# Sorting one batch's v in its natural layout and re-tiling it through DRAM

## The chip, the cores and the metric

The kernel runs on one core of a Trainium2 chip. The metric is the device time of one execution in microseconds. A core has five engines with instruction queues of their own: PE (matrix multiplication; PEld is its weight load), DVE (vector), ACT (scalar), POOL (which here builds a few masks and issues the loads) and SP (which here only issues DMAs). Sixteen DMA engines move the data. They serve two queues in this kernel: the one that POOL feeds (shown as q0, software_dynamic) and the one that SP feeds (q1, hardware_dynamic).

## The reference

Four batches of eight heads, 768 positions, head size 64. A small matrix per head is made doubly normalised (five rounds of exp, row sums, column sums) and mixes the eight 96-row blocks of k and of v; attention is then local to each block; the attended rows, all heads side by side (512 wide), go through a feed-forward layer with a squared ReLU.

```python
for _ in range(5):
    P = np.exp(P - P.max(-1, keepdims=True))
    P = P / (P.sum(-1, keepdims=True) + 1e-9)
    P = P / (P.sum(-2, keepdims=True) + 1e-9)
k_sorted = einsum('bhij,bhjcd->bhicd', P, k_b)     # k_b, v_b: 8 blocks of 96 rows
v_sorted = einsum('bhij,bhjcd->bhicd', P, v_b)
attn = softmax(q_b @ k_sorted^T / sqrt(64))        # within each block
x = (attn @ v_sorted), heads side by side          # 3072 x 512
out = relu(x @ w_in)**2 @ w_out                    # 512 -> 2048 -> 512
```

## The kernel before

**Work and batches.** The code counts batches from 0, so "the second batch" is `b == 1`. The attention of a batch runs in four units, one for each pair of heads (`hp` 0 to 3). The feed-forward layer (`ffn_unit`) runs in eight passes of 384 tokens, two for each batch: 64 "up" matmuls (L810, 128x384) in 16 chunks of four, each followed by a ReLU on ACT (L818) and a square on DVE (L821), and then 48 "down" matmuls (L838, 128x512) in 12 chunks of four, each third of them ending in a copy on ACT and a store.

**What a unit of batches 0 and 1 does.** `s_q` transposes q on PE (L461). `s_sort` sorts k and v by a matmul whose weights are the data (L510), which leaves both transposed. `s_sc` makes the scores (L550), ACT the exponentials. `s_vt` turns the sorted v back, so that positions lie on partitions, by eight 128x128 transposes on PE (L598) into `vs`, copied there by DVE. `s_av` multiplies by v (L731), and DVE divides by the sums (L741, L742) into `ao`. `s_xt` transposes the result into `xT`, for the first batch and the last unit of the second on PE (L779), otherwise by a transposing DMA from SP (L764).

**What batches 2 and 3 do.** `s_nat` sorts k and v by 32x32 tiles of PE: 16 matmuls (L632) for two pairs of heads, with weights `w_t` that `build_wt` makes (L406, L412, L419). The loads of k and v then have another layout (`kv_t`: 128 partitions with 1536 consecutive elements each, where the natural layout of `q_r`, `k_r`, `v_r` gives 384 elements in a run). The sorted v comes out with positions in the wrong place: it is copied to `vn`, written to DRAM (`v_way`, L656) and read back as `vblk` (L662), from where `s_av` takes it. The ring `rvb` has three such buffers, each for two units.

**The order.** `Plan` holds every operation with its engine, an assumed cost and its dependencies; `lay` and `lay_late` give the attention's PE operations due times in feed-forward chunks (`n_up` = 28 to a pass). `Plan.run` lists the operations, and each engine's queue is written in that order: PE, DVE, ACT and SP run theirs strictly in order. POOL's order is not written out by the plan; the tile framework sets it. Buffers of q, k and v (`ld` pool) are two of each, taken in turn: batch 2 gets those of batch 0, batch 3 those of batch 1, and a load waits until the last reader of its buffer is through. A load also waits for the eighth load before it.

```python
wr = plan.add("SP", 0.33, write, evs + [loaded(b)])
there = plan.add("WAY", 2.0, lambda e: None, [wr])
rd = plan.add("SP", 0.33, read, [there] + oldw)
back = plan.add("WAY", 2.0, lambda e: None, [rd])
```

Of the kernel before, what the change touches and what calls it, by code (L numbers as in the profile page):

```python
# [11 lines left out]
ALU = mybir.AluOpType  # L12
# [116 lines left out]
def kernel(  # L129
# [103 lines left out]
    for n in range(3):  # L233
        vb_r.append(const.tile([96, NB, HP, 66], BF16, name=f"vblk{n}"))
    v_way = nc.dram_tensor("v_way", (B, 2, NA, 128, HP * 66), BF16, kind="Internal").ap()

    kn_r = [const.tile([128, NA, 2, D], BF16, name=f"kn{n}") for n in range(3)]
    qi_r = [const.tile([128, NA, 2, D], BF16, name=f"qi{n}") for n in range(2)]
# [13 lines left out]
    xT = const.tile([128, KC, n_tok], BF16)  # L252
    w_all = const.tile([128, NH // 2, NB, C0], BF16)
    w_t = const.tile([128, NH // 4, 4, NB], BF16)
    qkv = {}
    landed = {}

# [9 lines left out]

    def alloc_qkv(b):
        if b not in qkv:
            qkv[b] = [ld.tile([128, H, NA * D], BF16, tag=t, name=t) for t in ("qb", "kb", "vb")]  # L270

    def load(b, t, h0, n, p=slice(0, 128)):
        def dst_src():
            alloc_qkv(b)
            if b > 1 and t:
                return (qkv[b][t].rearrange("p (g h) x -> p g (h x)", h=HP)[:, h0 // HP, :],
                        kv_t[t][b, :, h0 // HP, :])
            return qkv[b][t][p, h0:h0 + n, :], (q_r, k_r, v_r)[t][b, p, h0:h0 + n, :]
        dma((b, t, h0, p.start), 1.57 * n / H * (p.stop - p.start) / 128, dst_src,
            readers[b - 2] + [x_done[b - 1, x, 0] for x in range(HP)] if b > 1 else [])  # L280

    def load_w_in(g):
        f = slice(d_ff // 4 * g, d_ff // 4 * (g + 1))
# [23 lines left out]
    load_w_in(0)  # L307
    for g in range(1, 4):
        load_w_in(g)
    for g in range(4):  # L310
        t = slice(NT // 4 * g, NT // 4 * (g + 1))
        dma(("w_out", g), 1.05, lambda t=t: (w_out_bf[:, t, :], w_out_r[:, t, :]))
    for g in range(2):
        for t in (2, 1, 0):
            load(1, t, HP * g, HP)


    rs = const.tile([NH, NB], FP32)
# [83 lines left out]
    def build_wt(due):  # L402

        st = {}
        pick = const.tile([128, NB, 4], BF16, name="pick")
        picked = plan.add("DVE", 0.2, lambda e: nc.vector.tensor_copy(  # L406
            out=pick, in_=ident.rearrange("p (j c) -> p j c", c=C0)[:, :, 0:4]), [x_done[0, HP - 1, 0]])

        def mm(e):
            st["p"] = ps1.tile([128, NB, NH // 4], FP32, tag="p1", name="wtp")  # L410
            for h in range(4):
                nc.tensor.matmul(  # L412
                    out=st["p"][32 * h:32 * (h + 1), :, :].rearrange("p i g -> p (i g)"),
                    lhsT=pick.rearrange("p j c -> p (j c)"),
                    rhs=pt.rearrange("p i (g h) -> p h i g", h=4)[:, h, :, :],
                    start=True, stop=True)

        def fn(e):
            nc.vector.tensor_tensor(  # L419
                out=w_t,  # L420
                in0=mask_t[:, None, :, None].to_broadcast([128, NH // 4, 4, NB]),
                in1=st["p"].rearrange("p i g -> p g i")[:, :, None, :]
                .to_broadcast([128, NH // 4, 4, NB]),
                op=ALU.mult)

        s1, old = r1.take()
        pe = plan.add("PE", 0.15, mm, [cp, picked] + old, due, mode="col32")
        built["t"] = plan.add("DVE", 0.45, fn, [pe])
        r1.use(s1, pe, built["t"])


    class Unit:
# [184 lines left out]
    def s_nat(b, g, t, due):  # L617

        if t == 2:
            m, oldm = rvn.take()  # L620
        evs = []
        for hp in (2 * g, 2 * g + 1):
            slot, old = r2.take()
            if t == 1:
                m, oldm = rkn.take()

            def mm(e, hp=hp, slot=slot):
                src = qkv[b][t].rearrange("p (g h) x -> p g (h x)", h=HP)
                for h in range(2):
                    r = slice(32 * (2 * (hp % 2) + h), 32 * (2 * (hp % 2) + h + 1))  # L630
                    for c in range(4):
                        nc.tensor.matmul(  # L632
                            out=p2[slot][32 * c:32 * (c + 1), h, 0:NA * D],
                            lhsT=w_t[r, HP // 2 * b + g, :, :].rearrange("p c i -> p (c i)"),
                            rhs=src[r, g, NA * D * c:NA * D * (c + 1)],
                            start=True, stop=True, tile_position=(r.start, 32 * c))

            def ev(e, hp=hp, slot=slot, m=m):
                dst = (vn_r[m][:, :, 2 * (hp % 2):2 * (hp % 2) + 2, 0:D] if t == 2
                       else kn_r[m])  # L640
                copy(e, dst, p2[slot][:, :, 0:NA * D].rearrange("p e (a d) -> p a e d", d=D))

            pe = plan.add("PE", 0.15, mm, [landed[b, t, HP * g, 0], built["t"]] + old, due,
                          mode="tile")
            readers[b].append(pe)
            op = plan.add(AD, cost_f(2 * NA * D), ev, [pe] + oldm)
            r2.use(slot, pe, op)
            evs.append(op)
            if t == 1:
                rkn.use(m, op)  # L650
                k_nat[b, hp] = m, op
        if t == 1:
            return

        def write(e):
            nc.sync.dma_start(out=v_way[b, g].rearrange("a p x -> p a x"),  # L656
                              in_=vn_r[m].rearrange("p a h x -> p a (h x)"))

        w, oldw = rvb.take()

        def read(e):
            nc.sync.dma_start(  # L662
                out=vb_r[w].rearrange("p i h x -> p (i h x)"),
                in_=v_way[b, g].rearrange("a (c i) x -> (a c) (i x)", i=NB))

        wr = plan.add("SP", 0.33, write, evs + [loaded(b)])
        there = plan.add("WAY", 2.0, lambda e: None, [wr])
        rd = plan.add("SP", 0.33, read, [there] + oldw)
        back = plan.add("WAY", 2.0, lambda e: None, [rd])
        rvn.use(m, *evs, there)  # L670
        rvb.use(w, back)
        v_blk[b, g] = w, back
# [41 lines left out]

    def s_av(u, due=0):
        nao, olda = rao.take()
        if u.b > 1:
            w, u.vs_op = v_blk[u.b, u.hp // 2]
        u.norms = []
        for hf in u.halves:  # L720
# [4 lines left out]
            def mm(e, hf=hf, st=st, slot=slot):  # L725
                if hf == u.halves[0]:
                    u.ao = att.tile([96, u.ni, 2, D], BF16, tag="ao", name="ao", bufs=3)
                st["p"] = oup = p2[slot]
                for n in range(NQ):
                    for h in range(2):  # L730
                        nc.tensor.matmul(  # L731
                            out=oup[:, h, 66 * n:66 * n + D + 1],
                            lhsT=et_r[u.et[hf]][:, h, BLK * n:BLK * n + 128],
                            rhs=(u.vs[:, NQ * hf + n, h, 0:D + 1] if u.b < 2 else
                                 vb_r[w][:, NQ * hf + n, 2 * (u.hp % 2) + h, 0:D + 1]),
                            start=True, stop=True)

# [13 lines left out]
            op = plan.add("DVE", 0.9, norm, [pe])  # L751
            r2.use(s2, pe, op)
            ret.use(u.et[hf], pe)
            if u.b < 2:
                rks.use(u.n, pe)
            else:
                rvb.use(w, pe)
# [179 lines left out]
    def lay(b, halves, c0, c1):  # L937
        step, gap = (c1 - c0) / (HP + 0.9), (c1 - c0 - 13) / (HP - 1)
        for hp in range(HP):
            c = c0 + step * hp  # L940
            box = {}

            def open_(due, b=b, hp=hp, box=box):
                u = box["u"] = Unit(b, hp, halves)
                u.q_op = q2ops[hp] if b == 0 else s_q(b, hp, 0, 128, due)
                if b == 1:
                    build_w(H * b + 2 * hp, 2, pt, kops[b - 1, hp])
                u.k_op = kops[b, hp] = s_sort(u, 1, due)
                u.v_op = s_sort(u, 2, due)

            for f, s in ((0.0, open_),
                         (0.35, lambda due, box=box: s_sc(box["u"], due)),
                         (0.5, lambda due, box=box: s_vt(box["u"], due)),
                         (0.75, lambda due, box=box: s_av(box["u"], due)),
                         (1.2, lambda due, box=box: s_xt(box["u"], due))):
                todo.append((c + step * f, len(todo), s, b))

    def lay_late(b, c0):

        todo.append((c0, len(todo), lambda due: load_late(b), 0))  # L960
        if b == 2:
            todo.append((c0, len(todo), build_wt, 0))
        for g in range(2):
            for t in (1, 2):
                todo.append((c0 + 9 + 9 * g, len(todo),
# [17 lines left out]
                load(b, t, HP * g, HP)  # L983

    lay(0, (1,), 0, n_up)
    lay(1, (0, 1), n_up, 2 * n_up)
    lay_late(2, 2 * n_up)
    lay_late(3, 4 * n_up)
# [45 lines left out]
```

The softmax here doesn't subtract the row's maximum and nothing guards it: scores larger than these inputs give would overflow.

## Time and profile before

| what | value |
|---|---|
| median of 3 runs | 226.49 us (226.41 to 226.63) |
| the profiled execution's own time | 226.45 us |
| its span, first to last instruction | 224.3 us (2.15 us lie around it) |
| PE busy in the span | 216.6 us (97%) |
| PEld, ACT, DVE busy | 122.9, 122.1, 105.7 us |
| POOL busy | 26.4 us |
| granted PE clock | 1.00 throughout |
| DMA, mean over the span | 129 GB/s, 28.83 MB |

PE is busy in nearly all of the span; the other engines are busy for about half of it. The page cuts the span into 40 slices of 5.6 us; in its DMA row a 9 stands where the sixteen DMA engines are busy all the time. The first feed-forward pass begins at 22.3 us, the third (the first of the second batch) at 82.6 us. Between 49.4 and 82.5 us PE interleaves the second batch's attention with the second feed-forward pass.

### The profile page before, as it was taken

The numbers are of one execution on the slowest core, as the hardware profiler recorded it, in microseconds if no ns is written. First come the engines' busy times: TensorE is split into PE (matmuls) and PEld (weight loads), VectorE is DVE, ScalarE is ACT, GpSimd is POOL, SyncE is SP. The second block draws the span as 40 slices with busy tenths as digits, with TensorE's granted clock in tenths as the row PEclk, the third lists the DMA queues.
The fourth block names the chain that finished last, engine by engine and source line by source line (L and its number), as shares of the span: only waits on it lengthen the run. The fifth ranks groups of instructions, "written<-read, shape, count | busy, mean of one in ns | idle before, by whom it ended". The sixth has DMA issues, their size and how long they took to land.

```text
span 224.3 us, 5245 instructions
## 1 busy us (share of the span) xinstructions
PE 216.6 (97%) x2130; PEld 122.9 (55%) x2145; DVE 105.7 (47%) x297; ACT 122.1 (54%) x253; POOL 26.4 (12%) x46
## 2 busy tenths in 40 slices
PE   7898999999999999999999999999999999999994
PEld 2476665556665645545665455445665465446553
DVE  6777777317666416640666127523664045005400
ACT  4665776228885328734775248535774177137521
POOL 7962332200004200000000000000000000000000
PEclk9999999999999999999999999999999999999999
DMA  5999999999953996499941320899522410110012
GB/s 66 201 202 208 207 206 205 203 227 245 210 65 27 191 239 145 115 216 201 220 38 35 85 94 0 164 225 254 110 37 43 122 47 1 50 57 37 0 50 94
DMA packets 42744, 28.83 MB, mean 129 GB/s; under 512 B 22752, under 2 KB 38368, under 8 KB 42720
## 3 DMA queue, kind: packets, MB, share of 16 engines
q0 software_dynamic: 13888, 13.63, 37.1%
q1 hardware_dynamic: 28832, 14.86, 29.7%
q8 instruction: 17, 0.28, 0.5%
q14 instruction: 7, 0.06, 0.1%
HBM read 28.89 MB, written 7.91 MB: 164 GB/s over the span
## 4 chain that ended last, share of the span: by engine, by line
PE 92%; DMA 2%; DVE 2%; ACT 1%; issue 1%; ACTq 0%; POOLq 0%
PE hp L810 37%; PE op L838 35%; PE p L550 4%; PE p L731 3%; DMA qb<-in_q_dram 2%; PE p L510 2%; PE qtp L461 2%; PE vbp L598 2%; PE op L872 2%; PE p L350 1%; PE p L632 1%; PE xtp L779 1%; PE tp L510 1%; DVE ao L742 1%; ACT h L818 0%
## 5 line engine op out<-in xcount | busy, mean ns | idle before, releaser
L810 PE MATMUL hp<-xT,w_in_bf 128*128 128x384 bf16 x512 | 91.0, 326 | 0.0
L838 PE MATMUL op<-w_out_bf,h 128*128 128x512 bf16 x353 | 82.6, 379 | 0.8
L818 ACT ACTIVATE h<-hp 128x384 bf16<-128x384 f32 x128 | 62.0, 495 | 23.5 <-PE hp L810 20.0
L821 DVE TENSOR_TENSOR h<-h 128x384 bf16<-128x384 bf16 x128 | 44.5, 355 | 56.3 <-ACT h L818 55.5
L810 PEld LDWEIGHTS <-w_in_bf 128*128 128x128 bf16 x512 | 47.0, 98 | 30.0 <-issue 0.7
L838 PEld LDWEIGHTS <-h 128*128 128x128 bf16 x368 | 34.7, 98 | 39.4 <-issue 0.7
L192 ACT COPY ob<-op 128x512 f32<-128x512 f32 (+1 forms) x25 | 14.2, 569 | 56.0 <-PE op L838 50.6
L742 DVE TENSOR_TENSOR ao<-p,rec 96x512 bf16<-96x512 f32 x32 | 22.0, 687 | 1.4 <-DVE rec L741 0.3
L582 ACT ACTIVATE et<-p 96x384 bf16<-96x384 f32 x48 | 19.4, 491 | 2.4 <-PE p L550 2.4
L741 DVE RECIPROCAL rec<-p 96x8 f32<-96x8 f32 x32 | 6.4, 199 | 13.6 <-PE p L731 13.3
L731 PEld LDWEIGHTS <-et 96*128 96x128 bf16 x256 | 10.6, 97 | 2.9
L261 POOL DMA_DIRECT2D qb<-in_q_dram x8 | 6.0, 754 | 32.5 <-PE qtp L461 24.4
L350 PE MATMUL p<-ones 128*128 128x512 bf16 (+1 forms) x36 | 8.8, 360 | 1.1 <-DVE ones L213 1.1
L194 DVE COPY vs<-vbp 96x512 bf16<-96x512 bf16 (+1 forms) x12 | 6.1, 508 | 7.1 <-PE vbp L598 6.9
L573 ACT ACTIVATE et<-p 96x768 bf16<-96x768 f32 x8 | 6.3, 802 | 2.1 <-PE p L550 2.0
L261 POOL DMA_DIRECT2D kb<-in_k_dram x10 | 6.6, 659 | 6.6 <-DMA w_in_bf<-in_moe_w_in_dram 2.2
L261 POOL DMA_DIRECT2D vb<-in_v_dram x10 | 6.6, 660 | 6.4 <-DMA w_in_bf<-in_moe_w_in_dram 3.6
L192 ACT CAST ksT<-p 128x768 bf16<-128x768 f32 (+1 forms) x7 | 4.6, 662 | 3.3 <-PE p L510 3.3
L550 PEld LDWEIGHTS <-kx 64*128 64x128 bf16 x128 | 4.6, 155 | 2.8 <-issue 2.8
L731 PE MATMUL p<-vs,et 96*128 96x65 bf16 x128 | 6.0, 193 | 0.0
L461 PE MATMUL qtp<-ident,qb 64*64 64x64 bf16 (+1 forms) x144 | 4.7, 204 | 1.3 <-DMA qb<-in_q_dram 1.3
L461 PEld LDWEIGHTS <-qb 64*64 64x64 bf16 (+1 forms) x144 | 3.5, 109 | 4.5 <-DMA qb<-in_q_dram 2.3
(78 smaller groups left out, 129.3 us busy)
## 6 DMA issues: line engine op xcount, KB each, us to landing
out_dram<-ob SPq DMA_DIRECT2D x23, 256.0 KB, 2.8
qb<-in_q_dram POOLq DMA_DIRECT2D x8, 384.0 KB, 15.7
vb<-in_v_dram POOLq DMA_DIRECT2D x6, 384.0 KB, 17.1
kb<-in_k_dram POOLq DMA_DIRECT2D x6, 384.0 KB, 17.1
w_in_bf<-in_moe_w_in_dram POOLq DMA_DIRECT2D x4, 512.0 KB, 12.5
w_out_bf<-in_moe_w_out_dram POOLq DMA_DIRECT2D x4, 512.0 KB, 18.0
v_way<-vn SPq DMA_DIRECT2D x4, 396.0 KB, 4.1
vblk<-v_way SPq DMA_DIRECT2D x4, 396.0 KB, 3.9
```

Of the source, the lines that this page charges most:

```text
L192: nc.scalar.copy(out=out, in_=in_)
L261: nc.gpsimd.dma_start(out=dst, in_=src)
L350: nc.tensor.matmul(out=out, lhsT=ones, rhs=rhs, start=True, stop=True)
L461: nc.tensor.transpose(out=t["p"][64 * h:64 * (h + 1), a, :], in_=qb[p0:p1, 2 * hp + h, D * a:D * (a + 1)], identity=ident[p0:p1, p0:p1])
L550: nc.tensor.matmul(out=scp[:, h, BLK * n:BLK * (n + 1)], lhsT=(u.ksT[64 * h:64 * (h + 1), hf, BLK * n:BLK * n + 128] if u.b < 2 else kx_r[ ...
L582: nc.scalar.activation(out=et[:, h, 0:HS].rearrange("p (n c a) -> p n c a", c=C0, a=NA), in_=st["p"][0:96, h, 0:HS].rearrange("p (n a c) - ...
L731: nc.tensor.matmul(out=oup[:, h, 66 * n:66 * n + D + 1], lhsT=et_r[u.et[hf]][:, h, BLK * n:BLK * n + 128], rhs=(u.vs[:, NQ * hf + n, h, 0: ...
L742: nc.vector.tensor_tensor(out=u.ao[:, n0:n0 + NQ, :, :].rearrange("p n e d -> p e n d"), in0=ov[:, :, :, 0:D], in1=rec[:, :, :, None].to_b ...
L810: nc.tensor.matmul(out=t["hp", nt][:, 0:HS], lhsT=w_in_bf[:, kc, 128 * nt:128 * (nt + 1)], rhs=xT[:, kc, t0:t0 + HS], start=(kc == 0), sto ...
L818: nc.scalar.activation(out=t["h1", nt], in_=t["hp", nt][:, 0:HS], func=AF.Relu)
L821: nc.vector.tensor_tensor(out=t["h2"][:, nt, :], in0=t["h1", nt], in1=t["h1", nt], op=ALU.mult)
L838: nc.tensor.matmul(out=t["op", mt], lhsT=t["h2"][:, nt, 128 * mt:128 * (mt + 1)], rhs=w_out_bf[:, nt, :], start=(nt == 0), stop=(nt == NT ...
```

## The change

The second batch's v (its k stays as it was) goes the way of batches 2 and 3:

- `load`: v of batch 1 comes in the `kv_t` layout. Its first half is loaded between `w_in` and `w_out`, the rest of batch 1 in the order v, k, q, k, q after `w_out`.
- `build_wt` runs in the first feed-forward pass (it ran just before the third) and makes a second, small set of weights `w_v` for it (one more DVE instruction).
- `s_nat(1, g, 2)` runs for g = 0 and 1 in the first feed-forward pass, due in chunks 14 and 24. It replaces, in the four units of batch 1, the sort of v (`s_sort(u, 2)`) and `s_vt`.
- The sorted v is written to `v_nat` in DRAM by four DMAs for each g (32 partitions with 3168 bytes in one piece each) and read back to `vblk` by one DMA for each g (96 partitions x 8 pieces of 528 bytes). The plan assumes 6 us for each way, 2 us for the later batches' `v_way`.
- `s_av` of batch 1 takes v from `vblk`. The ring `rvb` now serves batches 1, 2 and 3.
- Buffers of q, k, v: batch 2 now takes those of batch 1 and batch 3 those of batch 0. In the built program POOL's queue has, after batch 1's loads, first the six loads of batch 3 (q, q, k, v, k, v), then batch 2's (v, v, q, q, k, k). Before, batch 2's six loads (q, q, k, v, k, v) stood ahead of batch 3's.

```diff
+    v_nat = nc.dram_tensor("v_nat", (B, 2, NB, BLK, HP * 66), BF16, kind="Internal").ap()
...
+    w_v = const.tile([128, 2, NB, 4], BF16)
...
     def alloc_qkv(b):
         if b not in qkv:
-            qkv[b] = [ld.tile([128, H, NA * D], BF16, tag=t, name=t) for t in ("qb", "kb", "vb")]
+            m = (b + 1) // 2 % 2
+            qkv[b] = [ld.tile([128, H, NA * D], BF16, tag=f"{t}{m}", name=t, bufs=1)
+                      for t in ("qb", "kb", "vb")]
...
-            if b > 1 and t:
+            if b > 1 and t or b == 1 and t == 2:
...
-            readers[b - 2] + [x_done[b - 1, x, 0] for x in range(HP)] if b > 1 else [])
+            readers[(0, 0, 1, 0)[b]] + [x_done[b - 1, x, 0] for x in range(HP)] if b > 1 else [])
...
+    load(1, 2, 0, HP)
     for g in range(4):
         t = slice(NT // 4 * g, NT // 4 * (g + 1))
         dma(("w_out", g), 1.05, lambda t=t: (w_out_bf[:, t, :], w_out_r[:, t, :]))
-    for g in range(2):
-        for t in (2, 1, 0):
-            load(1, t, HP * g, HP)
+    for t, g in ((2, 1), (1, 0), (0, 0), (1, 1), (0, 1)):
+        load(1, t, HP * g, HP)
...
+        built["v"] = plan.add("DVE", 0.25, fn1, [pe])
...
+                w = (w_v[:, g, :, :].rearrange("p i c -> p (i c)") if b == 1 else
+                     w_t[:, HP // 2 * b + g, :, :].rearrange("p c i -> p (c i)"))
...
+                            lhsT=w[r, :],
...
+            for c in range(4):
+                nc.sync.dma_start(
+                    out=v_nat[b, g].rearrange("i (y z a) x -> z (i y) (a x)", z=4, a=NA)[c],
+                    in_=vn_r[m][32 * c:32 * (c + 1)].rearrange("p a h x -> p (a h x)"))
...
+            if b == 1:
+                nc.sync.dma_start(
+                    out=vb_r[w].rearrange("p i h x -> p i (h x)"),
+                    in_=v_nat[b, g].rearrange("i p x -> p i x"))
+                return
...
-        wr = plan.add("SP", 0.33, write, evs + [loaded(b)])
-        there = plan.add("WAY", 2.0, lambda e: None, [wr])
+        wr = plan.add("SP", 0.33, write, evs + ([loaded(b)] if b > 1 else []))
+        slow = 6.0 if b == 1 else 2.0
+        there = plan.add("WAY", slow, lambda e: None, [wr])
...
-        if u.b > 1:
+        if u.b > 0:
             w, u.vs_op = v_blk[u.b, u.hp // 2]
...
-                u.v_op = s_sort(u, 2, due)
-
+                if b == 0:
+                    u.v_op = s_sort(u, 2, due)
+
+            if b == 1 and hp % 2 == 0:
+                todo.append((14 + 5 * hp, len(todo),
+                             lambda due, g=hp // 2: s_nat(1, g, 2, due), b))
...
-                         (0.5, lambda due, box=box: s_vt(box["u"], due)),
+                         (0.5, lambda due, box=box: b == 0 and s_vt(box["u"], due)),
...
-        if b == 2:
-            todo.append((c0, len(todo), build_wt, 0))
...
+    todo.append((8, len(todo), build_wt, 0))
```

More of the change, by code (lines that the diff above doesn't have):

```diff
@@ L424, in fn, with fn1 @@
                 op=ALU.mult)
+        def fn1(e):
+            nc.vector.tensor_tensor(
+                out=w_v,
+                in0=mask_t[:, None, None, :].to_broadcast([128, 2, NB, 4]),
+                in1=st["p"][:, :, 2:4].rearrange("p i g -> p g i")[:, :, :, None]
+                .to_broadcast([128, 2, NB, 4]),
+                op=ALU.mult)
         s1, old = r1.take()
         pe = plan.add("PE", 0.15, mm, [cp, picked] + old, due, mode="col32")
+        built["v"] = plan.add("DVE", 0.25, fn1, [pe])
         built["t"] = plan.add("DVE", 0.45, fn, [pe])
-        r1.use(s1, pe, built["t"])
+        r1.use(s1, pe, built["v"], built["t"])
     class Unit:
@@ L633, in mm @@
                             out=p2[slot][32 * c:32 * (c + 1), h, 0:NA * D],
-                            lhsT=w_t[r, HP // 2 * b + g, :, :].rearrange("p c i -> p (c i)"),
+                            lhsT=w[r, :],
                             rhs=src[r, g, NA * D * c:NA * D * (c + 1)],
@@ L655, in write @@
         def write(e):
-            nc.sync.dma_start(out=v_way[b, g].rearrange("a p x -> p a x"),
-                              in_=vn_r[m].rearrange("p a h x -> p a (h x)"))
+            if b > 1:
+                nc.sync.dma_start(out=v_way[b, g].rearrange("a p x -> p a x"),
+                                  in_=vn_r[m].rearrange("p a h x -> p a (h x)"))
+                return
[3 more added lines that the diff above has]
+                    in_=vn_r[m][32 * c:32 * (c + 1)].rearrange("p a h x -> p (a h x)"))
         w, oldw = rvb.take()
         def read(e):
+            if b == 1:
+                nc.sync.dma_start(
+                    out=vb_r[w].rearrange("p i h x -> p i (h x)"),
+                    in_=v_nat[b, g].rearrange("i p x -> p i x"))
+                return
             nc.sync.dma_start(
@@ L664, in read @@
                 in_=v_way[b, g].rearrange("a (c i) x -> (a c) (i x)", i=NB))
-        wr = plan.add("SP", 0.33, write, evs + [loaded(b)])
-        there = plan.add("WAY", 2.0, lambda e: None, [wr])
+        wr = plan.add("SP", 0.33, write, evs + ([loaded(b)] if b > 1 else []))
+        slow = 6.0 if b == 1 else 2.0
+        there = plan.add("WAY", slow, lambda e: None, [wr])
         rd = plan.add("SP", 0.33, read, [there] + oldw)
-        back = plan.add("WAY", 2.0, lambda e: None, [rd])
+        back = plan.add("WAY", slow, lambda e: None, [rd])
         rvn.use(m, *evs, there)
@@ L733, in mm @@
                             lhsT=et_r[u.et[hf]][:, h, BLK * n:BLK * n + 128],
-                            rhs=(u.vs[:, NQ * hf + n, h, 0:D + 1] if u.b < 2 else
+                            rhs=(u.vs[:, NQ * hf + n, h, 0:D + 1] if u.b < 1 else
                                  vb_r[w][:, NQ * hf + n, 2 * (u.hp % 2) + h, 0:D + 1]),
@@ L753, in s_av @@
             ret.use(u.et[hf], pe)
-            if u.b < 2:
+            if u.b < 1:
                 rks.use(u.n, pe)
```

## The prediction

> **What bounds the kernel now.** I read the busy row first, then the slices, then the chain of work that ended last.
>
> ```profile
> PE 216.6 (97%) x2130; PEld 122.9 (55%) x2145; DVE 105.7 (47%) x297; ACT 122.1 (54%) x253; POOL 26.4 (12%) x46
> PE   7898999999999999999999999999999999999994
> DMA  5999999999953996499941320899522410110012
> PE 92%; DMA 2%; DVE 2%; ACT 1%; issue 1%; ACTq 0%; POOLq 0%
> ```
>
> PE is the bound: from 22 us on it hardly idles, so PE time removed there comes off the end, and any wait of PE adds to it. But the DMA row is full of 9s for the first 11 slices, up to 62 us: this is where the change puts its way through DRAM. Next, PE in order of time over one unit of the second batch:
>
> ```profile
> 49.75 0.50 PE L510 MATMUL p<-w_all,kb 128*64 128x128 bf16 x12
> 50.08 0.50 PE L510 MATMUL p<-w_all,vb 128*64 128x128 bf16 x12
> 50.52 1.47 PE L810 MATMUL hp<-xT,w_in_bf 128*128 128x384 bf16 x8
> 51.92 0.51 PE L550 MATMUL p<-qT,ksT 64*128 64x96 bf16 x16
> 52.37 0.62 PE L598 MATMUL vbp<-ident,vsT 128*128 128x128 bf16 x8
> 52.83 1.46 PE L810 MATMUL hp<-xT,w_in_bf 128*128 128x384 bf16 x8
> ```
>
> The first column is the start; a step's cost is the distance to the next start (ends overlap). Last, the packets of the two queues in two short windows (queue: packets, MB, share of 16 engines), 46.5 to 47 us and 60.5 to 60.75 us:
>
> ```profile
> q1 hardware_dynamic: 51, 0.10, 61.0%
> q0 software_dynamic: 54, 0.04, 51.1%
> ...
> q0 software_dynamic: 18, 0.05, 93.7%
> q1 hardware_dynamic: 19, 0.00, 12.4%
> ```
>
> With both queues filled the packets alternate one to one, whatever their size: 2 KB stores (q1) with 768-byte loads, then 256-byte transposes (q1) with 3 KB loads.
>
> **PE time removed.** Sort of v: 50.08 to 50.52, 56.93 to 57.39, 64.00 to 64.46, 70.54 to 71.00. The first counts 0.33 only (k followed by v takes 0.33, k followed by feed-forward 0.44), so 0.33+3x0.46 = 1.71 us. Turning v back: 0.46, 0.45, 0.45, 0.67 (73.28 to 73.95); where the scores were followed by it directly (first and last unit) they took 0.45, followed by feed-forward 0.64, so 2.03-2x0.19 = 1.65 us. Together 3.36.
>
> **PE time added.** Two sorts by tiles: 16 such matmuls of batch 2 stood for 0.31 us (88.57 to 88.88) to 0.53, and the eight up matmuls ahead of them took 1.40 instead of 1.30; 0.42 each, 0.84 (up to 1.26). The weights' four matmuls (82.45 to 82.61) only move. By the built order the last unit's q and k no longer stand together: 0.1. Net 2.4; I take 2.3 (1.7 to 2.5), as the weights' PSUM buffer is now the one that the next `vbp` needs, behind two DVE steps (`w_t` 0.42, `w_v` less): up to 0.3 wait.
>
> **What is costed at nothing.** DVE and ACT lose four casts of `vsT` and four copies of `vs` (0.69 each) and get four casts of `vn` (0.96 on DVE, 0.80 on ACT); the first pass gets some 2.5 us more of both together, where each is busy for 11 of 15 us (22 to 37 us) and three PSUM buffers lie between them and PE; without that cover 0.3. `w_out` lands one load later, its last quarter at 39.5 instead of 37.6 us; the fourth chunk of down matmuls reads it at 41. Batch 2's loads now come last on POOL, q and k only after the second batch's q transposes and k sorts (70.0 and 70.3 before, some 72 to 75 in my case): keys land by 83, and the tile sort needs them 6 us into the third pass, at 90. SP's queue gets ten DMAs ahead of the second batch's transposes into `xT`; the third pass needs these at 82.6 before, 85 in my case.
>
> **The way through DRAM, the term that decides.** Per DMA engine, a 768-byte packet takes 0.059 us (1064 in 37.6 to 41.5 us over 16 engines), a 3 KB packet 0.24 (77 in 57 to 58 us, ten of them tiny), a small packet alone 0.029 (552 of 256 bytes in 65 to 66 us). A load is 32 packets per engine in natural layout (1.9 us) or 8 of 3 KB (1.9 us). A read of `v_nat` is 96x8/16 = 48 per engine: 1.4 us alone, 48x(0.059+0.029) = 4.2 beside natural loads, 48x(0.24+0.029) = 12.9 beside 3 KB loads. A DMA of SP issued into a full q0 also starts late: the store issued at 42.77 has its first packets after 46.0, and the three stores of that stretch take 5.3 to 6.5 us to land, where one at 128 us takes 2.8. I take 3.0 us to the first packet (rows 2.4 to 3.4).
>
> First half: `vn` is ready near 37, written by 44, the read is issued at 44, starts at 47 behind a store, lands at 52.5. Its `s_av` stood at 54.13; +1.0 (weights and two tile sorts), -0.33 and -0.27 removed ahead: 54.5. It fits by 2 us.
>
> Second half: `vn` is ready at 48; the write stands in SP's queue behind that read and a store, ends at 55, lands at 55.5; the read is issued at 56, first packets at 59. POOL's queue then: batch 1's last load lands near 52.5 (49.99 before, plus what SP's packets take), batch 3's two q by 59. Behind them stand six 3 KB loads without a break (batch 3's k, v, k, v, batch 2's v, v): 6x8 = 48 packets per engine, as many as the read has. Turn by turn both end together: 59 + 48x0.27 = 71.5 us. It cannot be much later, because q0's next loads wait for PE. The third unit's `s_av` needs it: 68.27 before, +1.0, -1.25 and -1.17 for three units' steps, -0.65 because one chunk less stands ahead of it: 66.2. PE, which runs in order, waits 5.3 us. With the 2.4 us start the read lands at 69.7 and the wait is 3.5. I take 4.6 (3.5 to 6), near the 3.0 row, three stores against one transpose. Behind the waiting matmul stand all feed-forward chunks.
>
> **A cold PE.** After such a wait PE may run slowly for a while. The trace has this only at its start: 512-column matmuls of 634 ns at first and 379 later, the first six or seven 0.43 us apart instead of 0.22, which loses 1.4 us. Later idle times are at most 1.34 us and cost nothing of the kind. So 0 to 1.4; I take 1.0, nearer to the row with a long idle time ahead. [...]
>
> [...] The two windows above show one to one in the trace's own packets, so my sum goes by the rows.
>
> **Sum.** Against the profiled execution's 226.45 us (its own span 224.3 and 2.15 around it; the median 226.49 is the same within 0.02%): -2.3 +4.6 +1.0 = 229.75; I say 229.7. A measurement of this kernel can tell about 0.2%, 0.45 us, from no change.
>
> **Rivals.**
> 1. The second read is in time (528-byte pieces take several to a turn, or q0 is a load further on). PE's saving stays: 226.45-2.3 = 224.1 (223.9 to 224.8). For it: the first read has this outcome by my own sum, and each us by which the read starts earlier, still beside natural loads, lets it land 3 us earlier (11 packets more, 0.27 each later). Against it: the alternation above and 48 packets each. It decides from a first packet before 57.5. Chance 0.23.
> 2. The read is nearly in time, but the transposes into `xT` (3x48 packets per engine, issued at 57 to 68, beside the same 3 KB loads) are the late ones: the first began 3.7 us after its issue and took 7.1 to land even with q0 about to run dry. Not stopped by an earlier wait, the third pass would need them at 80 while q0 stays full to 83: a wait of 1 to 3.5 us. 225.2 to 227.7, about no change. Chance 0.12, half of it within 0.2%.
> 3. My case with a bigger loss: batch 2's keys late as well, from the point where they land after 90 us instead of 83, or both reads late: 231 to 233. Chance 0.05.
>
> **How the numbers follow.** My case, 0.60: saving 1.7 to 2.5, wait 3.5 to 6, cold 0 to 1.4: its own range 227.5 to 231.6. With rival 1's 224.1 the range has to reach to 224.0, since leaving that case out loses 0.23; it leaves out most of rival 3 and the edges. Faster: rival 1 and a part of rival 2, 0.25. Same: 0.07. Slower: 0.60+0.05 and the rest of rival 2, 0.68.
>
> **What would show it.** Right: in the waits, PE at `s_av` of the second batch waits once for the DMA `vblk<-v_nat`, 3.5 to 6 us, near 66 us; that read takes 13 to 16 us to land, the other 8 to 9; the first 512-column matmuls after it are slower; the slices near 66 us show PE at 1 to 4. Then from the third pass on the timeline is that of before, shifted by 2 to 4 us. Wrong: both reads land in under 10 us and PE has no wait over 1 us (rival 1), or PE's wait stands at the first L839 up matmuls of the third pass (rival 2), or at the tile sort of k (rival 3).

## The result, and the profile after

The changed kernel takes **232.12 us** (median of four runs, 231.59 to 232.76); the kernel before takes 226.56 us beside it (226.41 to 226.92). The ratio is 1.0244, with a 95% interval of 1.0212 to 1.0276: slower by 5.6 us. The forecast was 229.7 us with a range from 224.0 to 231.6: the direction and the place of the wait are right, and the time lies 2.4 us above the forecast and 0.5 us above its range.

The profiled execution took 232.76 us; its span is 230.6 us. From the page: the busy row, the slices (5.77 us each), and the chain that ended last.

```profile
PE 219.4 (95%) x2097; PEld 121.5 (53%) x2097; DVE 103.7 (45%) x294; ACT 121.6 (53%) x253; POOL 26.0 (11%) x46
PE   8998999999955999999999999999999999999994
PEclk9999999999996799999999999999999999999999
DMA  5999999999997992079963221499921410011012
PE 79%; DMA 14%; DVE 3%; ACT 1%; issue 1%; SPq 1%; POOL 0%; ACTq 0%; DVEq 0%; POOLq 0%
```

PE has fewer instructions (2097 for 2130; the trace of before lacks 15 of its 368 down matmuls) but more busy time. Its row now has two 5s (63 to 75 us); the second of these slices and the one behind it have a lower granted clock. The DMA row is full up to 69 us, where it was full up to 62 before. The chain, almost all PE before, now goes through DMAs for 14%. PE's waits (total us, times, longest us):

```profile
PE p L760 <- DMA vblk<-v_nat: 5.2, 1, 5.2
PE p L355 <- DVE ones L213: 1.1, 1, 1.1
```

The second wait stands at the kernel's start, as before. The first is the new one. The timeline of PE (start, us): one unit of the second batch, the place of the wait, and the start of the third pass:

```profile
51.59 0.50 PE L524 MATMUL p<-w_all,kb 128*64 128x128 bf16 x12
52.03 1.48 PE L839 MATMUL hp<-xT,w_in_bf 128*128 128x384 bf16 x8
53.43 0.51 PE L564 MATMUL p<-qT,ksT 64*128 64x96 bf16 x16
53.88 1.47 PE L839 MATMUL hp<-xT,w_in_bf 128*128 128x384 bf16 x8
...
65.14 1.47 PE L839 MATMUL hp<-xT,w_in_bf 128*128 128x384 bf16 x8
71.85 1.04 PE L760 MATMUL p<-vblk,et 96*128 96x65 bf16 x16 [5.23 <-DMA vblk<-v_nat]
72.82 0.85 PE L475 MATMUL qtp<-ident,qb 128*64 128x128 bf16 x12
73.60 1.46 PE L839 MATMUL hp<-xT,w_in_bf 128*128 128x384 bf16 x4
74.85 1.91 PE L867 MATMUL op<-w_out_bf,h 128*128 128x512 bf16 x4
...
88.72 6.01 PE L839 MATMUL hp<-xT,w_in_bf 128*128 128x384 bf16 x36
```

In the unit the sort of v behind that of k and the eight transposes behind the scores are gone. `s_av` of the third unit (L760) begins at 71.85 us, after the second read of `v_nat`. The four up matmuls behind it take 1.46 us, where eight took 1.47 before the wait. The third pass begins at 88.72 us (82.61 before). From there to the end it is 141.9 us, and 141.7 before: all that changed lies ahead of it.

Packets of the two queues while the read waits, from 63 to 64 us (queue: packets, MB, share of 16 engines):

```profile
q0 software_dynamic: 59, 0.18, 88.1%
q1 hardware_dynamic: 58, 0.03, 14.6%
```

And from 71 to 72 us, when q0 has run dry (only q1 is listed, and what it moves by then are mostly the 256-byte packets of the transposes into `xT`):

```profile
q1 hardware_dynamic: 747, 0.19, 89.8%
```

58 of the read's 528-byte packets in a microsecond beside 59 of POOL's loads, 747 small ones alone: one to one, as in the windows of before (51 to 54, 19 to 18). Equal numbers alone would also come of longer turns of equal length; the start times of the packets decide it. From 63 to 68.5 us the commonest distance between the starts of two 3 KB packets is 0.266 us. From 60.9 to 62.3 us, when SP's queue moves nothing, it is 0.229 us. So between two 3 KB packets there are 0.037 us more: room for one small packet (58 of them in 14.6% of 16 us are 0.040 us each), and no more.

### The profile page after: what moved, and what is told of

It is laid out like the page before. It is cut to its first block, busy times and chain, and to the rows that moved or that the text cites. A ratio compares the mean times of both kernels' runs of the same rounds, so it can differ in the third digit from the quotient of the medians.

```text
span 230.6 us, 5180 instructions
## 1 busy us (share of the span) xinstructions
PE 219.4 (95%) x2097; PEld 121.5 (53%) x2097; DVE 103.7 (45%) x294; ACT 121.6 (53%) x253; POOL 26.0 (11%) x46
## 4 chain that ended last, share of the span: by engine, by line
PE 79%; DMA 14%; DVE 3%; ACT 1%; issue 1%; SPq 1%; POOL 0%; ACTq 0%; DVEq 0%; POOLq 0%
PE op L867 33%; PE hp L839 31%; DMA vblk<-v_nat 5%; DMA v_nat<-vn 4%; PE p L564 3%; PE p L760 3%; DMA qb<-in_q_dram 3%; DMA kx<-kn 2%; PE p L649 2%; PE op L901 2%; DVE ao L771 1%; PE p L524 1%; PE vbp L612 1%; PE qtp L475 1%; PE xtp L808 1%
## 5 line engine op out<-in xcount | busy, mean ns | idle before, releaser
L867 PE MATMUL op<-w_out_bf,h 128*128 128x512 bf16 x368 | 85.0, 383 | 0.0
L847 ACT ACTIVATE h<-hp 128x384 bf16<-128x384 f32 x128 | 61.3, 497 | 23.1 <-PE hp L839 18.8
L850 DVE TENSOR_TENSOR h<-h 128x384 bf16<-128x384 bf16 x128 | 44.2, 355 | 62.3 <-ACT h L847 61.2
L192 ACT COPY ob<-op 128x512 f32<-128x512 f32 (+1 forms) x24 | 13.6, 567 | 56.3 <-PE op L867 53.7
L760 PEld LDWEIGHTS <-et 96*128 96x128 bf16 x256 | 10.9, 99 | 8.5 <-issue 5.6
L760 PE MATMUL p<-vblk,et 96*128 96x65 bf16 x192 | 8.5, 197 | 5.3 <-DMA vblk<-v_nat 5.2
L355 PE MATMUL p<-ones 128*128 128x512 bf16 (+1 forms) x36 | 10.0, 399 | 1.1 <-DVE ones L213 1.1
L192 ACT COPY qT<-qtp 128x384 bf16<-128x384 bf16 (+1 forms) x11 | 5.7, 555 | 6.5 <-PE qtp L475 6.5
L263 POOL DMA_DIRECT2D vb<-in_v_dram x10 | 6.1, 613 | 10.3 <-DMA qb<-in_q_dram 4.1
L194 DVE CAST vn<-p 128x768 bf16<-128x768 f32 x6 | 5.7, 958 | 2.1 <-PE p L649 1.9
L564 PE MATMUL p<-qT,kx 64*128 64x96 bf16 x128 | 5.6, 226 | 0.0
L724 DVE COPY qi<-qb 128x768 bf16<-128x768 bf16 x8 | 2.7, 356 | 6.4 <-DMA qT<-qi 6.4
```

Of the source, the lines that this page charges most:

```text
L192: nc.scalar.copy(out=out, in_=in_)
L263: nc.gpsimd.dma_start(out=dst, in_=src)
L355: nc.tensor.matmul(out=out, lhsT=ones, rhs=rhs, start=True, stop=True)
L564: nc.tensor.matmul(out=scp[:, h, BLK * n:BLK * (n + 1)], lhsT=(u.ksT[64 * h:64 * (h + 1), hf, BLK * n:BLK * n + 128] if u.b < 2 else kx_r[ ...
L760: nc.tensor.matmul(out=oup[:, h, 66 * n:66 * n + D + 1], lhsT=et_r[u.et[hf]][:, h, BLK * n:BLK * n + 128], rhs=(u.vs[:, NQ * hf + n, h, 0: ...
L847: nc.scalar.activation(out=t["h1", nt], in_=t["hp", nt][:, 0:HS], func=AF.Relu)
```

## The experiments

The theory: two losses. PE waits 5.4 us for the second read, because six 3 KB loads stand in q0 beside it; and the clock that falls during this wait (0.50 for 6.83 us) costs more after it. The rivals: the clock costs nothing beyond the wait (the rest is another wait or the buffers' exchange); and the read is slow by itself.

**e2: keep PE busy in the wait.** 24 matmuls of 512 columns, whose result nobody reads, ahead of the waiting `s_av`.

```diff
+                if u.b == 1 and u.hp == 2 and hf == 0:
+                    fill(8.0, slot)
```

> Changed kernel with 24 dummy 512-column matmuls on PE (5.2 us, on data that nobody reads) ahead of the third unit's s_av, where PE waited 5.2 us for the read of v_nat. My theory (PE's wait costs 5.4 us, and the 6.83 us at half clock behind it another 3.4): the read lands when it did, near 71.7 us, PE's granted clock stays 1.00, time 232.1-3.4 = 228.7 us (228.2 to 229.2). Rival, the clock after the wait costs little and the rest of the loss lies elsewhere (the third pass's transposes, the loads of batch 2): 231 to 232.

Measured: 229.69 us (229.53 to 230.03), ratio 1.0143 (1.0128 to 1.0159). PE's timeline:

```profile
66.42 5.34 PE L355 MATMUL p<-ones 128*128 128x512 bf16 x24
71.60 0.66 PE L762 MATMUL p<-vblk,et 96*128 96x65 bf16 x16
72.65 0.82 PE L841 MATMUL hp<-xT,w_in_bf 128*128 128x384 bf16 x4
```

The read lands hardly earlier (71.49 us for 71.71), and `s_av` begins almost as late as in the changed kernel (71.60 us for 71.85), but the next four up matmuls take 0.82 us instead of 1.46, the granted clock is 1.00, and the third pass begins at 85.63 us. Useless work in the wait makes the kernel 2.4 us faster. In the profiled runs, `s_av` to the third pass took 16.87 us in the changed kernel and 14.03 here, so 2.8 us there are the clock. The 2.4 us by the medians are the price of the clock, less a wait of 0.2 us for `xT` that comes up at the third pass; the expected 228.7 was 1 us too low, since I had put this price at 3.4 us.

**e3: no second read.** The third and fourth unit take v from the first read's tile.

```diff
+            if b == 1 and g == 1:
+                return
...
-                                 vb_r[w][:, NQ * hf + n, 2 * (u.hp % 2) + h, 0:D + 1]),
+                                 vb_r[v_blk[1, 0][0] if u.b == 1 else w][:, NQ * hf + n, 2 * (u.hp % 2) + h, 0:D + 1]),
```

> Changed kernel without the second read of v_nat; units 2 and 3 of the second batch take v from the first read's tile instead (so half of that batch's v is not the right one). My theory: no wait at s_av, no slow clock. With the second read's place in SP's queue taken by the transposes into xT, these share the 3 KB loads turn by turn (48 packets each at 0.27 us) and the last lands at 82 to 84 us, where the third pass needs it at 80: PE waits 2 to 4 us there, 226 to 228 us in all. Rival, only the read's own chain through DRAM was late and the transposes keep their time: no wait of PE at all, 226.45-2.6 = 223.9 us.

Measured: 225.92 us (225.54 to 226.4), ratio 0.9976 (0.9964 to 0.9988). PE's timeline at `s_av` and at the third pass:

```profile
66.43 0.73 PE L762 MATMUL p<-vblk,et 96*128 96x65 bf16 x16
...
80.53 0.49 PE L841 MATMUL hp<-xT,w_in_bf 128*128 128x384 bf16 x2
82.11 5.69 PE L841 MATMUL hp<-xT,w_in_bf 128*128 128x384 bf16 x34 [1.09 <-DMA xT<-ao]
```

Without the wait the third pass begins at 80.53 us. That is 2.08 us earlier than before the change: the PE work saved, free of all waits. Then a second wait shows that the first had covered: the last transposes into `xT`, issued at 68.74 us, land at 82.07, beside batch 2's q and k loads, of which the first is issued at 67.92 us here and at 73.97 in the changed kernel. So the read alone is worth 6.2 us, and under it lies 1.1 us more.

**e4: POOL in the planner's order.** The loads of batches 2 and 3 are issued where the planner lists them, batch 2 ahead of batch 3; the first that waits for a sort of the second batch holds all others.

```diff
-        mybir.EngineType.SP}))
+        mybir.EngineType.SP, mybir.EngineType.Pool}))
```

> Changed kernel with POOL's queue in the plan's order too: batch 2's loads (k first) come right behind batch 1's and wait for the last k sort of batch 1 near 69 us, batch 3's follow. POOL's load queue is then empty from about 53 to 70 us. My theory (3 KB loads beside the second read make it late): the read lands within 5 us of its issue, before 64 us, PE has no wait over 0.5 us, clock 1.00, time 226.45-2.6 = 223.9 us (223.5 to 224.6). Rival, the chain of write and read through DRAM is too long by itself: PE still waits over 2 us at s_av, 226 us or more. Second rival, batch 2's keys now land too late: PE waits at the tile sort of k near 86 us.

Measured: 234.22 us (233.81 to 234.78), ratio 1.0343 (1.0324 to 1.0362). The read is issued at 54.33 us and lands at 57.82: 3.5 us, so it is not slow by itself, and `s_av` does not wait. But the loads that had stood beside it now run to 101 us and stand beside the DMAs that batch 2 issues from SP. From the timelines of PE and DVE:

```profile
103.19 0.52 PE L649 MATMUL p<-vb,w_t 32*32 32x384 bf16 x8 [7.94 <-DVE kn L194]
...
102.18 0.96 DVE L194 CAST kn<-p 128x768 bf16<-128x768 f32 x1 [9.30 <-DMA kx<-kn]
```

PE waits for DVE's copy into `kn`, which frees the buffer that PE writes next, and that copy waits for the buffer `kn`, which a transposing DMA into `kx` still reads: issued at 90.20 us, landed at 102.09, behind the write into `v_way` (89.77 to 101.45) in SP's queue. The theory of the read held, the expected time did not, and neither rival came: `s_av` has no wait, and the tile sort of k at 86.51 us has none. The collision had moved to the next small-packet transfers, and the clock loss with it (0.5 for 10.24 us from 98.60).

**e5: the read in large pieces.** `v_nat` laid out so that the read has 4224 bytes in a piece (four DMAs), and the write has 528; the order of the weights `w_v` and the write follow from that (not shown).

```diff
-    v_nat = nc.dram_tensor("v_nat", (B, 2, NB, BLK, HP * 66), BF16, kind="Internal").ap()
+    v_nat = nc.dram_tensor("v_nat", (B, 2, BLK // 4, 4, NB, HP * 66), BF16, kind="Internal").ap()
...
+                for y in range(4):
+                    nc.sync.dma_start(
+                        out=vb_r[w][24 * y:24 * (y + 1)].rearrange("p i h x -> p (i h x)"),
+                        in_=v_nat[b, g].rearrange("t y i x -> y t (i x)")[y])
```

> Changed kernel with v_nat laid out so that the reads come in pieces of 4224 bytes (8 packets on each of 12 engines, by four DMAs) and the writes in pieces of 528 bytes; the small packets thus lie in the writes, beside 768-byte loads. My theory (one packet per turn whatever its size): the second read takes 4 to 7 us to land instead of 12.6, lands at 63 to 66 us, PE's wait at s_av is under 1 us. The transposes into xT still share the 3 KB loads and may make the third pass wait up to 3 us: 224 to 227 us. Rival, the bytes or the two hops through DRAM make the read late, not its number of packets: still lands after 69 us, 229 us or more.

Measured: 233.96 us (233.68 to 234.23), ratio 1.0326 (1.0309 to 1.0343): a miss. PE's waits:

```profile
PE p L761 <- DMA vblk<-v_nat: 6.6, 1, 6.6
```

Packets from 60 to 61 us, while the second write is under way:

```profile
q0 software_dynamic: 66, 0.19, 94.5%
q1 hardware_dynamic: 64, 0.04, 16.3%
```

The small pieces are now the write's, and they alternate with the loads just as the read's did; the write, which I had expected beside 768-byte loads, meets the 3 KB ones, and the read is issued only at 65.92 us. The rival's numbers came (a landing after 69 us, over 229 us), but not for its reason: in e4 the same bytes take the same two ways through DRAM, and the read needs 3.5 us. The way has 48 small packets per engine at one of its ends, and whichever end meets the loads pays.

**e6, e7, e8: POOL's order by hand.** One edit, in which only the list differs: the loads of batches 2 and 3 are issued in this order, each once the last readers of its buffer have been issued. The parts not shown put POOL among the engines whose order is written out and give q, k and v of a batch their buffers one by one.

```diff
+    made, queue = set(), [(3, 0, 0), (3, 0, 1), (2, 2, 0), (2, 2, 1), (2, 0, 0), (2, 0, 1),
+                          (2, 1, 0), (2, 1, 1), (3, 1, 0), (3, 2, 0), (3, 1, 1), (3, 2, 1)]
...
+        while queue:
+            b, t, g = queue[0]
+            if not all(r in made for r in reads[3 - b if b == 2 else 0, t] + reads["loads"]):
+                break
+            late[queue.pop(0)](None)
```

The triples are batch, tensor (q, k, v) and half. This list is that of e6: batch 3's k and v last, so that two 3 KB loads without a wait (batch 2's v) stand beside the read. e7 leaves four there (batch 3's k, v, k, v; batch 2's v last). e8 has the changed kernel's order, with all six: it shows what writing the order by hand does.

> Changed kernel with batch 3's four 3 KB loads (k, v, k, v) moved to the end of POOL's queue, by an order of POOL written out by hand: batch 1; batch 3's q, q; batch 2's v, v, q, q, k, k; then batch 3's k, v, k, v. The other engines' orders stay. My theory (the second read's 48 packets per engine take one turn each with q0's packets, 3 KB ones above all): only two 3 KB loads lie beside the read, it lands near 64 us, before its s_av at 66.4; PE has no wait over 0.5 us, clock 1.00, the third pass starts at 80.5 us; span 222.3, time 224.4 us (224.1 to 225.0). Rival, moving them only moves the loss, as when POOL's queue went by the plan: the four loads then run at 78 to 90 us and meet the third pass's write of v_way and its transposes: a PE wait of over 2 us at 90 to 100 us, 226.5 us or more.

> Changed kernel with only batch 2's two v loads moved to the end of POOL's queue, so that four 3 KB loads instead of six stand beside the second read. My theory: q0 runs dry near 67 us and the read lands near 68 instead of 71.7; PE waits 1.5 us (0.8 to 2.5) at s_av, too short for the clock to fall: granted clock 1.00; time 224.4+1.5 = 225.9 us (225.2 to 227.0). Rival, the number of loads does not matter (the read has a long latency of its own): lands after 70 us, half clock, 230 us or more.

> Control: the changed kernel with POOL's order written out by hand in the way of the two runs beside it, but in the very order that it has anyway. All theories: as the changed kernel, 231.6 to 232.8 us, with the 5.4 us wait and the half clock.

| 3 KB loads beside the read | time (range), us | ratio (interval) | read landed | wait at `s_av` |
|---|---|---|---|---|
| two (e6) | 224.72 (224.65 to 225.05) | 0.9929 (0.9916 to 0.9941) | 64.05 us | none |
| four (e7) | 227.19 (226.44 to 229.93) | 1.0046 (1.0015 to 1.0077) | 67.63 us | 1.2 us |
| six (e8) | 231.32 (231.0 to 231.63) | 1.0216 (1.0198 to 1.0235) | 71.43 us | 5.0 us |

Each pair of loads taken away lets the read land 3.6 to 3.8 us earlier: about the 1.9 us of each load. Timeline of e6 at `s_av` and the third pass:

```profile
66.32 0.73 PE L768 MATMUL p<-vblk,et 96*128 96x65 bf16 x16
...
80.42 0.49 PE L847 MATMUL hp<-xT,w_in_bf 128*128 128x384 bf16 x2
81.58 5.68 PE L847 MATMUL hp<-xT,w_in_bf 128*128 128x384 bf16 x34 [0.67 <-DMA xT<-ao]
```

and of e7, the same places:

```profile
67.76 0.66 PE L768 MATMUL p<-vblk,et 96*128 96x65 bf16 x16 [1.22 <-DMA vblk<-v_nat]
...
83.56 5.68 PE L847 MATMUL hp<-xT,w_in_bf 128*128 128x384 bf16 x34 [1.28 <-DMA xT<-ao]
```

e6's time came out as expected, and it beats both kernels, the one before by 0.7%: it has the saving and pays only 0.7 us at `xT`, where I had expected no wait over 0.5. The loss did not move on as in e4, though only just: the four loads moved to the end land by 90.29 us, and the next write into `v_way` is issued at 90.45. e7's wait at `s_av` was as expected; its time was 1.3 us more, for the transposes into `xT`, which I had not counted. After a wait of 1.2 us the clock stays at 1.00 in e7's profiled run; two of its nine runs, at 229.68 and 229.93 us, show a mean clock of 0.992 and 0.993. e8 is 0.8 us below the changed kernel and 0.3 us below what was expected, with nearly the same wait (5.0 us for 5.2); its clock fell for half as long, which is taken up below.

**e1: the buffers back.** Batch 2 loads into batch 0's buffers and batch 3 into batch 1's; POOL's queue has loads of the same sizes in the same places.

```diff
-            m = (b + 1) // 2 % 2
+            m = b % 2
...
-            readers[(0, 0, 1, 0)[b]] + [x_done[b - 1, x, 0] for x in range(HP)] if b > 1 else [])
+            readers[b - 2] + [x_done[b - 1, x, 0] for x in range(HP)] if b > 1 else [])
```

> Changed kernel with batch 2 again in the first batch's buffers and batch 3 in the second's; POOL's queue then has batch 2's q, q, k, v, k, v, then batch 3's v, v, q, q, k, k: the same sizes in the same places with the batches exchanged. My theory (the size and place of the loads beside the read count, not whose they are): as the changed kernel, 231.5 to 233 us, wait 5 to 5.6 us. Rival, the new place of the batches' buffers is a cause by itself: below 230 us.

Measured: 231.05 us (230.6 and 231.49), ratio 1.0204 (1.0186 to 1.0223), with a wait of 5.0 us (5.2 in the changed kernel); the read landed at 71.41 us. That is half a microsecond under the expected range and one above the rival's 230: wait and landing stay, so the exchange of the buffers is not what costs. What counts is how many loads stand in q0, not whose buffer they fill.

## Why the prediction was wrong, point by point

Each term, forecast against measured, on the profiled executions:

| term | forecast, us | measured, us | from |
|---|---|---|---|
| profiled execution before | 226.45 | 226.45 | |
| PE's saving | -2.3 (1.7 to 2.5) | -2.1 | third pass without a wait at 80.53 (e3), 82.61 before |
| wait for the second read | +4.6 (3.5 to 6) | +5.4 | `s_av` at 71.85, without the wait at 66.45 |
| cold PE | +1.0 (0 to 1.4) | +2.8 | third pass 8.19 later than in e3, of which 5.40 is the wait; `s_av` to third pass 16.87, with the clock at 1.00 14.10 (e3) and 14.03 (e2) |
| from the third pass on | 0 | +0.2 | 141.9 for 141.7 |
| sum | 229.75 | 232.75 | measured 232.76 |

**The step that failed is the cold PE: the term was mis-sized, and its upper bound of 1.4 us was too low.** It was read from the kernel's start, the only place in the trace of before with slow matmuls, and that was a short draw: the 12 matmuls with which PE begins there, always at 1.06 us, took 4.11 us in the trace of before, the least of all ten traces, and 5.30 in the changed kernel's. What the runs show in its place is the granted clock, in stretches of the trace (us, PE busy, PEld, DVE, ACT, POOL, granted clock, DMA share, GB/s). In the changed kernel:

```profile
68.00:71.30 3.30, 0.00 (x0) 0.00 (x0) 0.00 (x0) 0.00 (x0) 0.00 (x0) 1.00 1.17 201
71.40:74.80 3.40, 2.95 (x32) 2.10 (x33) 2.18 (x7) 0.80 (x1) 0.83 (x2) 0.50 0.41 79
74.80:78.10 3.30, 3.30 (x19) 1.34 (x18) 0.68 (x3) 1.00 (x2) 0.92 (x2) 0.50 0.82 94
78.20:81.60 3.40, 3.40 (x30) 1.56 (x29) 0.43 (x1) 1.76 (x5) 0.73 (x2) 1.00 1.32 218
```

In e8, with nearly the same wait:

```profile
71.90:75.20 3.30, 3.30 (x29) 1.86 (x26) 2.54 (x8) 1.29 (x2) 1.50 (x2) 0.50 0.23 33
75.30:78.60 3.30, 3.30 (x40) 1.57 (x39) 0.22 (x1) 0.94 (x2) 1.08 (x2) 1.00 0.99 144
```

The clock falls to 0.50 and comes back in steps of 3.41 us: two of them in the changed kernel (71.36 to 78.19 us), in e1 (69.65 to 76.48) and in e5 (71.88 to 78.71), one in e8 (71.84 to 75.25), three in e4 (98.60 to 108.84). In the changed kernel PE starts again at 71.85, half a microsecond after a step has begun: that step is not busy throughout, and the next is cold too. In e8 PE starts at 71.57, just before a step begins, and one is enough. In the changed kernel, in e1 and in e8, then, the clock is low after PE's new start for one whole step (3.41 us) and for what is left of the low step in which PE starts (2.93 us, 1.52 us, and nothing in e8, where it had not yet fallen). After PE's new start the clock was low for 6.34 us in the changed kernel, 4.93 in e1 and 3.41 in e8; the loss, by the third pass's start (88.72, 87.78, 87.14 us against 80.53, or 80.42 of e6 for e8) less the wait, was 2.8, 2.1 and 1.5 us: 0.43 to 0.44 us for each cold microsecond in all three. For one to two steps my estimate from this is 1.5 to 2.9 us, depending on where in a step PE starts; the forecast's 1.4 was just short of the least. The range was short in another way too: the bounds of the case, 226.45-1.7+6+1.4, add up to 232.15, not to the 231.6 at which it ended.

**The wait was right in kind and 0.8 us too small; that the landing was right is in part luck.** The read was issued at 59.08 us, not 56, since the last of the second write's four DMAs (issued at 50.15 us) landed at 58.94 while the other three had by 56.81. Its first packet came at 62.55 us, not 59. Yet it landed at 71.71 us, where 71.5 was forecast. The forecast's own sum, 59 + 48x0.27, gives 72.0, and from 62.55 it would have given 75.5. What set the landing was the end of the loads, the bound that the forecast had named ("It cannot be much later"): the last of the six landed at 71.34, after some 33 turns beside the read, and what was left of the read ran alone at the end. In e8 the read is issued 1.5 us earlier, at 57.58 us, and lands with its loads all the same (71.43, the last load 71.21). From issue to landing it took 12.6 us, and the first read 9.5, where 13 to 16 and 8 to 9 had been named as signs. The forecast had 71.5 in its working and then shaded the wait down to 4.6 for an earlier start. With its own 5.3 the sum would have been 230.45.

**The saving was right** (2.1 for 2.3), and so, as to what PE waited for, were the first read (landed 54.23 us, 1.7 later than forecast, but before `s_av` at 55.19), `w_out` (39.43) and batch 2's keys (85.50 at the latest, their sort at 94.66). Costing these at nothing held.

**The rivals.** The first (the read in time) came about only with other orders of POOL's queue, in e4 and e6. Several small pieces to a turn, the first of its two grounds, is not what the packets show: 59 of the loads to 58 of the read, 66 to 64 in e5, and the 0.266 us from one 3 KB packet to the next leave room for one small packet. The second (transposes into `xT` late) was forecast as an alternative to the wait; e3, e6 and e7 show a wait there as the next one behind it, of 0.7 to 1.3 us. Its cause is another than the six loads named: in e3 the first two transposes, beside those, landed by 72.17 us, and the late one is the last, beside batch 2's q and k. The third did not occur: the keys were in time, and the bigger loss came from the clock.

## What to carry to other kernels

A transfer of many small pieces that must land by a certain time is to be costed by what stands in the other queues beside it: here each of its packets let one 3 KB packet pass, so it ended when the loads ran out (a read issued 1.5 us earlier, in e8, landed only 0.3 us earlier). Moving four loads that nobody needed soon from ahead of it to behind it was worth 6.6 us (e8 to e6), and making its pieces larger at one end only moved the collision to the other. A wait of PE of some 5 us should be priced with the cold clock behind it, 1.5 to 2.8 us more here, and the next wait under it should be looked for before a gain is counted.

## What had not been expected of the hardware

- The half clock comes in steps of 3.41 us whose phase decides the price: nearly the same wait (5.2, 5.0 and 5.0 us) cost 2.8, 2.1 and 1.5 us behind it. Matmuls that do nothing useful in the wait kept the clock at 1.00 and were worth 2.4 us (e2). The changed kernel's four runs (231.59 to 232.76) all have a mean clock of 0.985, as the profiled one with its two steps; that their scatter is this phase too was not shown.
- A DMA issued by SP while q0 is full begins late: the second read, issued at 59.08 us, has its first packet at 62.55, 3.5 us later, and in e8 it is 3.5 us too (57.58 and 61.11). With q0 empty it is 1.0 us, and 3.5 us from issue to landing (e4). The store ahead of the read in SP's queue had its last packet at 60.51 us, so for 2 us the queue moved nothing. Where these pass, no run tells.
